# 42 of 128 attention heads with token-major scores, weights turned by DMA, and value products emitted four iterations later

## The chip, the core and the metric

The kernel runs on one NeuronCore of a Trainium2 chip. The metric is the device time of one execution in microseconds (us), the median of three runs; the profile comes from one more execution with the hardware profiler on.

TensorE (PE) multiplies; its weight loads are listed apart as PEld. ScalarE (ACT) evaluates functions, VectorE (DVE) does elementwise work, GpSimd (POOL) a little more of that, and SyncE (SP) issues nearly all DMAs. Each engine works its instructions off in the order in which the program emits them, and waits where a semaphore has not yet been reached.

## What is computed

The reference is one transformer block with adaptive layer norm. x has 2048 tokens of 1024 features; there are 32 query heads and 4 key/value heads of 128 features; keys and values are the last 512 of a cache of 2048.

```
mod = silu(c) @ w_mod                         # six vectors: sa, ca, ga, sb, cb, gb
h = layernorm(x) * (1 + ca) + sa
q = h @ wq                                    # 32 heads
p = softmax(q @ k.T * 128 ** -0.5)            # k, v: last 512 cached, one for 8 query heads
x = x + ga * ((p @ v) @ wo)
h = layernorm(x) * (1 + cb) + sb
x = x + gb * ((silu(h @ w_gate) * (h @ w_up)) @ w_down)      # 3584 wide
```

All matrices are bf16.

## The kernel before

The tokens are worked off in four chunks of 512. The attention loop (line 903) has a counter i that runs over chunk and head together: 128 heads in all, number n being head n mod 32 of chunk n div 32. It is a software pipeline written out by hand. Iteration i emits

- `qproj(i+3)` (L641): eight matmuls of 512 columns into PSUM bank 4, then a VectorE cast of the result to bf16 (L644),
- `scores(i-1)` (L805): four matmuls with 128 keys stationary and 512 queries moving, into banks 0 to 3, so that the scores lie keys by queries; then two exponentials of 128x1024 on ScalarE (L813) into one of two buffers `ex_s`,
- `pv(i-2)` (L816): 16 matmuls of 129 columns, with 128 keys x 128 queries of the exponentials stationary and 128 value columns plus a column of ones moving. The column of ones gives the sums. VectorE takes their reciprocal (L831) and multiplies (L834); a DMA transpose of 128x512 (L837) puts the head's output, features by tokens, into `oT_all`,
- one step of background work (`run_bg`): the layer norm of the next chunk, with a DMA transpose of 128x1024 for each 128 tokens (L454).

When the last head of a chunk is through, `oproj` (L870) multiplies `oT_all` by wo: eight groups of 32 matmuls, with the residual added by VectorE through two buffers `tmp` (L853, L855). Tables of iteration numbers (LOADX, LOADO, LOADT and so on, from L891) say when loads and small steps are issued; `LOADT` issues 24 DMA transposes of columns of w_mod (L588), and `load_wq` the 1 MB of weights for the next four heads. After the attention come the feed-forward layers, untouched by the change.

Waits are not written by hand. Every instruction goes through `T.op` (L55), which looks at the buffers (`_Buf`) that it reads and writes: a reader waits for the buffer's last write, and a writer for its last write and the reads since then. "Last" is by the order in which the program emits. The instruction that waits holds up its engine's queue.

All matrix products of the kernel go through a helper at L271.

Of the kernel before, what the change touches and what calls it, by code (L numbers as in the profile page):

```python
# [7 lines left out]
P = 128  # L8
# [122 lines left out]
def bass_adaLN_cond__sliding_block_cached__swiglu_ffn__prompt_kernel(  # L131
# [63 lines left out]
    rstd = [rstd4[:, i:i + 1] for i in range(4)]  # L195
    bq = S_("bq", [P, 8], F32)
    rl = [S_("rl%d" % i, [P, 4], F32) for i in range(2)]
    nsc = [S_("nsc%d" % i, [P, D], BF16) for i in range(2)]
    tmp = [S_("tmp%d" % i, [P, 512], F32) for i in range(2)]

    KB = 1024
    A_BYTES = 162 * KB
# [19 lines left out]
    def bank(b, n=512, off=0):  # L222
        return ps[:, b * 512 + off:b * 512 + off + n]
# [19 lines left out]
    B_mv = [_Buf("mv%d" % i) for i in range(4)]  # L243
    B_rs = [_Buf("rs%d" % i) for i in range(4)]
    B_rl = [_Buf("rl%d" % i) for i in range(2)]
    B_ns = [_Buf("ns%d" % i) for i in range(2)]
    B_tmp = [_Buf("tmp%d" % i) for i in range(2)]
    B_h2 = [[_Buf("h2_%d_%d" % (s, dt)) for dt in range(DT)] for s in range(2)]
# [12 lines left out]
    with nc.Block() as block:  # L261

        @block.gpsimd
        def _(g):
# [5 lines left out]
            def mm(out_ap, lhsT, rhs, start, stop, reads, bank_buf, skip=False):  # L270
                T.op(PE, lambda: TE.matmul(out_ap, lhsT, rhs, start=start, stop=stop, skip_group_check=skip),  # L271
                     reads=reads, writes=[bank_buf])
# [368 lines left out]
            def qproj(i, b=QB, k0=0):  # L641
                qproj_mm(i, b, k0, DT)
                qs = q_slot(i)
                T.op(DVE, lambda: V.tensor_copy(qT_s[qs], bank(b)), writes=[PB[b], B_qT[qs]])  # L644
# [160 lines left out]
            def scores(i):  # L805
                ch, h = divmod(i, Hq)
                gk = h // rep
                qs = q_slot(i)
                es = i % NEX
                for kt in range(KT):  # L810
                    mm(bank(SCB + kt), kT_sb[:, gk * KT + kt, :], qT_s[qs], True, True, [B_kT[gk], B_qT[qs]], PB[SCB + kt])
                for kp in range(KT // 2):
                    T.op(ACT, lambda: A.activation(ex_s[es][:, 2 * kp:2 * kp + 2, :], banks2(SCB + 2 * kp), AF.Exp, scale=att_scale),  # L813
                         writes=[PB[SCB + 2 * kp], PB[SCB + 2 * kp + 1], B_ex[es]])

            def pv(i):  # L816
                ch, h = divmod(i, Hq)
                gk = h // rep
                es = i % NEX
                os_ = i % NOS  # L820

                for jj in range(2):
                    for kt in range(KT):
                        for jb in range(2):
                            j = 2 * jb + jj
                            b = PVB + jb
                            mm(bank(b, P + 1, jj * 130), ex_s[es][:, kt, j * P:(j + 1) * P], v_aug[:, gk * KT + kt, 0:P + 1],
                               kt == 0, kt == KT - 1, [B_ex[es], B_va, B_vg[gk]], PB[b])
                both = [PB[PVB], PB[PVB + 1]]
                r = i % 2  # L830
                T.op(DVE, lambda: V.reciprocal(rl[r][:, :].rearrange("p (a b) -> p a b", a=2), psap(PVB * 512 + P, [[512, 2], [130, 2]])),  # L831
                     writes=both + [B_rl[r]])
                rlb = bass.AP(tensor=rl[r][:, :].tensor, offset=0, ap=[[4, P], [2, 2], [1, 2], [0, P]])
                T.op(DVE, lambda: V.tensor_tensor(o_s[os_].rearrange("p (a b) d -> p a b d", a=2),  # L834
                                                  psap(PVB * 512, [[512, 2], [130, 2], [1, P]]), rlb, ALU.mult),
                     reads=[B_rl[r]], writes=both + [B_os[os_]])
                T.op(Q_tr[os_], lambda: SP.dma_start_transpose(oT_all[:, h, :].rearrange("p (j q) -> p j q", j=TPC),  # L837
                                                               o_s[os_].rearrange("p j d -> p (j d)")),
                     reads=[B_os[os_]], writes=[B_oT[h]])

            B_wo = [_Buf("wo%d" % i) for i in range(8)]
            wo_s = [None] * 8
# [21 lines left out]
            def oproj_end(ch, k, b):  # L864
                j, hf = divmod(k, 2)
                t = ch * TPC + j
                resid(b, t, hf * 512, 512, 0, k, x_res[:, t, :], B_x[t])
                run_bg(1)

            def oproj(ch):  # L870
                for k in range(2 * TPC):
                    b = [QB, XB][k % 2]
                    oproj_mm(ch, k, b, 0, Hq)
                    oproj_end(ch, k, b)

            ln1 = {}
            ln2 = {}
# [15 lines left out]
            GATER = {19 + n: NGP + n for n in range(DT - NGP)}  # L893
            GATET = {23: 0, 24: 1}
            GATES = {26: 0, 27: 1}
            t2 = Hq + 6 + (9 * (NL - 1)) // 4
            TURNT = (28, t2 + 1)
            PUTT = {33: (0, c_sil, B_csil), 30: (1, mrow[0:DT, :], B_mrow), t2 + 3: (2, mrow[0:DT, :], B_mrow)}
            GETT = {35: (0, sc_row, B_scr), 31: (1, rowb[0][:, :], B_row[0]), t2 + 4: (2, rowb[1][:, :], B_row[1])}
            LOADT = {Hq + 2 + (9 * n) // 4: n for n in range(NL)}  # L900
            LOADO = {5 + (21 * p) // 8: p for p in range(8)}
            LOADK = {1: 1, 5: 2, 6: 3}
            for i in range(1, NA + 2):
                ch, h = divmod(i, Hq)
                if i in LOADK:
                    load_k(LOADK[i])
                if i == 4:
                    load_wq((i + 4) // 4 + 1)
                if 2 <= i < NQ0:
                    q_shifted(i)  # L910
                if i in (2, 3):
                    load_wga(i - 2)
                if i in LOADX:
                    load_x(LOADX[i])
                if i in LOADO:
                    load_wo(LOADO[i])
                if i in GATET:
                    gate_turn(GATET[i])
                if i in TURNT:
                    if i > Hq:  # L920
                        T.op(DVE, lambda: V.tensor_copy(mstg[:, 0:DT], mcol[:, 2 * DT:3 * DT]), reads=[B_mcol], writes=[B_mstg])
                    row_turn()
                if i in PUTT:
                    row_put(*PUTT[i])
                if i in GETT:
                    row_get(*GETT[i])
                if i == 7:
                    add_ln1(1)
                if h == 2 and 1 <= ch < NCH - 1:
                    add_ln1(ch + 1)  # L930
                if h == 2 and ch == NCH - 1:
                    add_ln2(0)
                if i + LEAD < NA:
                    if (i + LEAD) % Hq == 0:
                        finish(ln1[(i + LEAD) // Hq])
                    if i == 1:
                        scores(0)
                    if i in (1, 3, 5):
                        q_bias_mm(i + 1, i + 3, XB)
                    if i > NQ0:  # L940
                        qproj(i + LEAD)
                    elif i % 2 == 1:
                        qproj_mm(NQ0 + i // 2, QB, 0, HK)
                    else:
                        qproj(NQ0 - 1 + i // 2, QB, HK)
                if i - 4 in LOADT:
                    n = LOADT[i - 4]
                    mod_col(n)
                    g0, last = divmod(n, DT)
                    if last == DT - 1:  # L950
                        mod_take(g0, B_late[g0 + 1])
                        if g0 == 1:
                            mod_gain(1, B_late[2], B_g[1])
                n = i - (NA - LEAD)
                if 0 <= n <= 2:
                    oproj_mm(NCH - 1, 0, QB, 8 * n, 8 * n + 8)
                elif n >= 3:
                    oproj_mm(NCH - 1, 1, XB, 8 * (n - 3), 8 * (n - 3) + 8)
                if 1 <= i - 1 < NA:
                    scores(i - 1)  # L960
                if 0 <= i - 2 < NA:
                    pv(i - 2)
                    ch2, h2 = divmod(i - 2, Hq)
                    if i % 4 == 1 and i > 5:
                        load_wq((i + 4) // 4 + 1)
                    if i in LOADT:
                        load_mt(LOADT[i])
                    if h2 == Hq - 1 and ch2 < NCH - 1:
                        oproj(ch2)
                run_bg(1)  # L970
                for n in GATEP.get(i, ()):
                    gate_part(n)
                if i in GATER:
                    gate_row(GATER[i])
                if i in GATES:
                    gate_sum(GATES[i])
                if i == max(GATER):
                    gate_split()
# [152 lines left out]
```

## Time and profile before

| | before |
|---|---|
| median of 3 runs | 1270.05 us (1269.99 to 1270.45) |
| the profiled execution, its own time | 1270.14 us |
| its span, first to last instruction | 1268.3 us |
| TensorE busy | 1255.1 us (99%) |
| VectorE busy | 485.1 us (38%) |
| ScalarE busy | 341.6 us (27%) |
| DMA transposes of heads (128x512), to landing, median | 2.6 us |
| DMA transposes of the layer norm (128x1024), to landing, median | 5.1 us |

The profile is a page and answers drawn from the same trace. A line of a group reads: source line, engine, operation, out<-in by the program's names, shapes, count; then busy time and mean time of one in ns; then the idle time of the engine just before, with what ended it. A timeline line reads: start and duration in us, engine, line, operation, count, and in brackets the idle time before it. Of a DMA the line gives the duration of its issue on the queue (SPq is SyncE's), and apart from that the time from issue to landing. Matmuls are pipelined, so their mean durations are longer than their distance. A few matmul records can be missing.

### The profile page before, as it was taken

To read this page: it belongs to the slowest core of one execution; us is meant where nothing else is said; L and a number is where in the kernel's file an instruction comes from. 1 tells how busy PE (TensorE), PEld (TensorE's weight loads), DVE (VectorE), ACT (ScalarE), POOL (GpSimd) and SP (SyncE) were. 2 spreads that over 40 slices of the span, in tenths; PEclk is the share of its full clock that TensorE was granted. 3 is DMA by queue.
4 is the path that set the end of the run, shared out by engine and by line. 5 is a ranking of instruction groups with operands and counts; after the bars stand their busy time and mean duration, and the time that the engine had idled before them with its cause. 6 is when DMAs were issued, how large, how long until landed. Compare 5 with 4: busy or idle time off the path is not lost.

```text
span 1268.3 us, 17609 instructions
## 1 busy us (share of the span) xinstructions
PE 1255.1 (99%) x7442; PEld 640.7 (51%) x7583; DVE 485.1 (38%) x894; ACT 341.6 (27%) x389; POOL 56.0 (4%) x95
## 2 busy tenths in 40 slices
PE   8999999999999999999999999999999999999999
PEld 5655545555455554555544444444444444444444
DVE  4676226764257641365322321233212321222122
ACT  4655205553035550155510111011100111011100
POOL 1530000000000000000000000000000000000000
PEclk9999999999999999999999999999999999999999
DMA  9998306875029641064243972055512644034200
GB/s 320 264 263 218 92 1 127 177 171 125 1 57 177 138 114 34 9 129 123 61 145 100 291 246 94 25 158 150 168 40 72 177 141 134 17 128 154 67 9 25
DMA packets 239997, 156.67 MB, mean 124 GB/s; under 512 B 133296, under 2 KB 225840, under 8 KB 239920
## 3 DMA queue, kind: packets, MB, share of 16 engines
q1 hardware_dynamic: 181664, 96.83, 31.6%
q10 hardware_dynamic: 58256, 58.73, 14.6%
q8 instruction: 59, 0.97, 0.3%
q14 instruction: 18, 0.15, 0.1%
HBM read 119.93 MB, written 4.20 MB: 98 GB/s over the span
## 4 chain that ended last, share of the span: by engine, by line
PE 98%; issue 1%; DMA 0%; SPq 0%; DVE 0%
PE ps L271 98%; DMA arena<-in_w_mod_dram 0%; SPq L309 0%; SPq L334 0%; PE ps L275 0%; DVE arena L496 0%; DVE tmp L853 0%; DVE arena L855 0%; DVE gain_f L486 0%
## 5 line engine op out<-in xcount | busy, mean ns | idle before, releaser
L271 PE MATMUL ps<-arena 128*128 128x512 bf16 (+1 forms) x7213 | 1249.3, 333 | 10.1 <-POOL arena L298 2.0
L271 PEld LDWEIGHTS ps<-arena 128*128 128x128 bf16 x7354 | 632.9, 98 | 621.5 <-issue 2.1
L813 ACT ACTIVATE arena<-ps 128x1024 bf16<-128x1024 f32 x256 | 261.9, 1023 | 345.1 <-PE ps L271 333.4
L1059 ACT ACTIVATE arena<-ps 128x512 bf16<-128x512 f32 x112 | 66.9, 597 | 499.6 <-PE ps L271 499.6
L1060 DVE TENSOR_TENSOR arena<-ps,arena 128x512 bf16<-128x512 f32 x112 | 77.5, 692 | 276.2 <-PE ps L271 276.2
L853 DVE TENSOR_TENSOR tmp<-ps,rowb 128x512 f32<-128x512 f32 (+1 forms) x65 | 44.4, 683 | 318.8 <-PE ps L271 318.8
L644 DVE CAST arena<-ps 128x512 bf16<-128x512 f32 x120 | 82.8, 690 | 47.7 <-PE ps L271 47.7
L834 DVE TENSOR_TENSOR arena<-ps,rl 128x512 bf16<-128x512 f32 x128 | 88.5, 691 | 4.7 <-DVE rl L831 0.2
L831 DVE RECIPROCAL rl<-ps 128x4 f32<-128x4 f32 x128 | 23.4, 182 | 114.1 <-PE ps L271 114.1
L429 POOL TENSOR_SCALAR rstd<-mv 128x1 f32<-128x1 f32 x28 | 6.1, 216 | 910.3 <-DVE mv L428 910.3
L424 DVE BATCH_NORM_STATS2 st<-x_res 128x6 f32<-128x512 bf16 x62 | 42.4, 683 | 3.4 <-DMA x_res<-in_A_x_dram 3.3
L593 DVE SCALAR_TENSOR_TENSOR arena<-arena 128x1024 bf16<-128x1024 bf16 x24 | 29.2, 1215 | 0.0
L855 DVE TENSOR_TENSOR arena<-tmp,x_res 128x512 bf16<-128x512 f32 (+2 forms) x33 | 22.3, 677 | 1.1
L855 DVE TENSOR_TENSOR x_res<-tmp,x_res 128x512 bf16<-128x512 f32 x32 | 22.2, 693 | 1.1
L440 DVE TENSOR_SCALAR arena<-arena,gain,mod_bf 128x512 bf16<-128x512 bf16 x56 | 21.2, 420 | 0.0
L435 DVE TENSOR_SCALAR nsc<-x_res,mv,rstd 128x1024 bf16<-128x1024 bf16 x30 | 19.2, 641 | 0.0
L431 POOL TENSOR_TENSOR rstd<-rstd,mhalf 128x1 f32<-128x1 f32 x28 | 15.7, 559 | 2.3
L772 POOL TENSOR_SCALAR arena<-arena,sc_bf 128x512 f32<-128x512 bf16 x8 | 12.9, 1614 | 0.5 <-POOL arena L774 0.2
L774 POOL TENSOR_TENSOR arena<-arena 128x512 f32<-128x512 f32 x8 | 10.1, 1265 | 0.7
L428 DVE BATCH_NORM_AGGREGATE mv<-st 128x2 f32<-128x12 f32 x28 | 5.8, 209 | 1.0
L271 PEld LDWEIGHTS ps<-sc_bf,arena 128*128 128x128 bf16 x128 | 4.4, 96 | 1.4 <-DMA arena<-in_w_mod_dram 0.3
L271 PE MATMUL ps<-sc_bf,arena 128*128 128x1 bf16 x128 | 4.7, 164 | 0.3 <-DMA arena<-in_w_mod_dram 0.3
(56 smaller groups left out, 59.4 us busy)
## 6 DMA issues: line engine op xcount, KB each, us to landing
arena<-in_A_wq_dram SPq DMA_DIRECT2D x30, 1024.0 KB, 5.8
arena<-in_B_w_gate_dram ACTq DMA_DIRECT2D x28, 1024.0 KB, 5.4
arena<-in_B_w_up_dram ACTq DMA_DIRECT2D x28, 1024.0 KB, 7.9
arena<-in_A_wo_dram SPq DMA_DIRECT2D x8, 1024.0 KB, 7.6
arena<-in_B_w_down_dram SPq DMA_DIRECT2D x7, 1024.0 KB, 8.3
out_dram<-arena SPq DMA_DIRECT2D x15, 256.0 KB, 2.0
x_res<-in_A_x_dram SPq DMA_DIRECT2D x3, 1024.0 KB, 7.0
arena<-arena SPq DMA_TRANSPOSE x132, 2.6
```

Source lines behind the costliest of these rows:

```text
L271: T.op(PE, lambda: TE.matmul(out_ap, lhsT, rhs, start=start, stop=stop, skip_group_check=skip), reads=reads, writes=[bank_buf])
L424: T.op(DVE, lambda: V.bn_stats(st_[sl][:, hf * 6:hf * 6 + 6], x_res[:, t, hf * 512:hf * 512 + 512]), reads=[B_x[t]], writes=[B_st[sl]])
L440: T.op(DVE, lambda: V.tensor_scalar(dst[:, dt, :], dst[:, dt, :], gain[gi][:, dt:dt + 1], mod_bf[:, ccol + dt:ccol + dt + 1], op0=ALU.mult ...
L593: T.op(DVE, lambda: V.scalar_tensor_tensor(mt[n % 2], mt[n % 2], 1.0, sc_row, op0=ALU.mult, op1=ALU.mult, accum_out=mcol[:, n:n + 1]), rea ...
L644: T.op(DVE, lambda: V.tensor_copy(qT_s[qs], bank(b)), writes=[PB[b], B_qT[qs]])
L813: T.op(ACT, lambda: A.activation(ex_s[es][:, 2 * kp:2 * kp + 2, :], banks2(SCB + 2 * kp), AF.Exp, scale=att_scale), writes=[PB[SCB + 2 * k ...
L831: T.op(DVE, lambda: V.reciprocal(rl[r][:, :].rearrange("p (a b) -> p a b", a=2), psap(PVB * 512 + P, [[512, 2], [130, 2]])), writes=both + ...
L834: T.op(DVE, lambda: V.tensor_tensor(o_s[os_].rearrange("p (a b) d -> p a b d", a=2), psap(PVB * 512, [[512, 2], [130, 2], [1, P]]), rlb, A ...
L853: T.op(DVE, lambda: V.tensor_tensor(tmp[s][:, 0:n], bank(b, n), rowb[ri][:, c0:c0 + n], ALU.mult), reads=[B_row[ri]], writes=[PB[b], B_tmp ...
L855: T.op(DVE, lambda: V.tensor_tensor(dst[:, c0:c0 + n], tmp[s][:, 0:n], x_res[:, t, c0:c0 + n], ALU.add), reads=[B_tmp[s], B_x[t]], writes= ...
L1059: T.op(ACT, lambda: A.activation(sg_s[ss], bank(gb), AF.Silu), writes=[PB[gb], B_sg[ss]])
L1060: T.op(DVE, lambda: V.tensor_tensor(guT[:, ft, :], bank(ub), sg_s[ss], ALU.mult), reads=[B_sg[ss]], writes=[PB[ub], B_gu[ft]])
```

## The change

42 of the 128 heads take another form: numbers 34, 36 to 54, and 66, 68 to 126. All are even; the odd ones between them stay as they were.

For such a head (`nat_scores`) the queries are stationary and 512 keys move, so the scores lie queries by keys. Four exponentials of 128x512 write the buffer `pn[s]` and, with an accumulator, the sums of each row. `nat_norm` takes reciprocals and multiplies in place, in two halves. `nat_turn` issues one DMA transpose of 128x2048 from `pn[s]` to `pt[s]`. `nat_pv` then has the values stationary and 512 queries moving: four matmuls, whose result is already features by tokens; ScalarE copies it to `oT_all`. There are two slots: `p_slot(i) = (i - 34) // 2 % 2`. Slot 0 of `pn` lies where `ex_s[0]` lay, slot 1 is the `tmp` pair of the residual. The slots of `pt` lie in a region that changes at heads 34, 66, 86 and 96 (`PTAT`).

In the loop, `nat_scores(i+1)` and the first half of its `nat_norm` stand in the odd iteration i, the second half and `nat_turn` in the next one, and `nat_pv(i-4)` behind that. At a chunk's end what is left is flushed before `oproj`. Heads 34, 66 and 98 have their scores and normalisation between groups of `oproj`. `load_wq` moves ahead of the scores from iteration 33 on, the w_mod transposes go to every second iteration (from nine in four), and the background step moves ahead of `nat_scores` in odd iterations.

```diff
+            NAT0 = Hq + 2
+            NAT = set(range(NAT0, 2 * Hq - 8, 2)) | set(range(2 * Hq + 2, NA, 2))
+            B_pn = [[_Buf("pn0_%d" % hf) for hf in range(2)], B_tmp]
+            pn = [None, tmp_t[:, :].bitcast(BF16)]
...
+            def p_slot(i):
+                return (i - NAT0) // 2 % 2
...
+            def nat_scores(i):
...
+                for j in range(TPC):
+                    mm(bank(SCB + j), qT_s[qs][:, j * P:(j + 1) * P],
+                       kT_sb[:, gk * KT:(gk + 1) * KT, :].rearrange("p a b -> p (a b)"), True, True,
+                       [B_kT[gk], B_qT[qs]], PB[SCB + j])
+                for j in range(TPC):
+                    T.op(ACT, lambda: A.activation(pn[s][:, j * 512:(j + 1) * 512], bank(SCB + j), AF.Exp, scale=att_scale,
+                                                   accum_out=psum[s][:, j:j + 1]),
+                         writes=[PB[SCB + j], B_pn[s][j // 2], B_psum[s][j // 2]])
+            def nat_norm(i, hf):
+                s = p_slot(i)
+                T.op(DVE, lambda: V.reciprocal(pinv[s][:, 2 * hf:2 * hf + 2], psum[s][:, 2 * hf:2 * hf + 2]),
+                     reads=[B_psum[s][hf]], writes=[B_pinv[s][hf]])
+                for j in (2 * hf, 2 * hf + 1):
+                    pj = pn[s][:, j * 512:(j + 1) * 512]
+                    T.op(DVE, lambda: V.tensor_scalar(pj, pj, pinv[s][:, j:j + 1], None, op0=ALU.mult),
+                         reads=[B_pinv[s][hf]], writes=[B_pn[s][hf]])
+            def nat_turn(i):
+                s = p_slot(i)
+                pt_of[i] = (pt[s], B_pt[s], list(pt_over))
+                T.op(Q_pt[s], lambda: SP.dma_start_transpose(pt[s], pn[s]), reads=B_pn[s], writes=[B_pt[s]])
+            def nat_pv(i):
...
+                pa, pb, over = pt_of.pop(i)
+                ptv = pa.rearrange("p (j k) q -> p j k q", j=TPC)
+                for kt in range(KT):
+                    mm(bank(PVB).rearrange("p (j q) -> p j q", j=TPC), v_aug[:, gk * KT + kt, 0:P], ptv[:, :, kt, :],
+                       kt == 0, kt == KT - 1, [B_va, B_vg[gk], pb], PB[PVB])
+                T.op(ACT, lambda: A.activation(oT_all[:, h, :], bank(PVB), AF.Copy), writes=[PB[PVB], B_oT[h]])
...
+            PTAT = {NAT0: OFF_OT + 24 * KB, 2 * Hq + 2: OFF_OT + 24 * KB, 2 * Hq + 22: OFF_H20, 3 * Hq: OFF_HT}
...
+                if i % 4 == 1 and i >= NAT0 - 1:
+                    load_wq((i + 4) // 4 + 1)
...
+                seam = (i - 1) % Hq == 0 and i + 1 in NAT
+                if i + 1 in PTAT and not seam:
+                    pt_region(PTAT[i + 1])
+                if i in NAT and (i - 2) % Hq:
+                    nat_norm(i, 1)
+                    nat_turn(i)
+                nat = i % 2 == 1 and i + 1 in NAT
+                if nat and not seam:
+                    if i - 4 not in LOADT:
+                        run_bg(1)
+                    nat_scores(i + 1)
+                if 1 <= i - 1 < NA and i - 1 not in NAT:
                     scores(i - 1)
                 if 0 <= i - 2 < NA:
-                    pv(i - 2)
+                    if i - 4 in pt_of:
+                        nat_pv(i - 4)
+                    if i - 2 not in NAT:
+                        pv(i - 2)
+                    if (i - 2) % Hq == Hq - 1 or i == NA:
+                        for n in sorted(pt_of):
+                            if n < i:
+                                nat_pv(n)
+                    if nat and not seam:
+                        nat_norm(i + 1, 0)
...
                     if h2 == Hq - 1 and ch2 < NCH - 1:
-                        oproj(ch2)
+                        oproj(ch2, [lambda: nat_scores(i + 1), lambda: (nat_norm(i + 1, 0), nat_norm(i + 1, 1))] if seam else ())
+                        if seam:
+                            if i + 1 in PTAT:
+                                pt_region(PTAT[i + 1])
+                            nat_turn(i + 1)
```

## The prediction

> **What bounds the kernel now.** I read the page's busy table first, then its chain of waits, then the timeline of two quiet iterations of the attention loop.
>
> ```profile
> span 1268.3 us, 17609 instructions
> ...
> PE 1255.1 (99%) x7442; PEld 640.7 (51%) x7583; DVE 485.1 (38%) x894; ACT 341.6 (27%) x389; POOL 56.0 (4%) x95
> ...
> PE 98%; issue 1%; DMA 0%; SPq 0%; DVE 0%
> ```
>
> TensorE is busy for 99% of the span and carries 98% of the chain: it never waits in the attention loop. So an edit gains only by giving TensorE less to do, and every wait put on TensorE's queue is paid in full. The timeline gives the pace.
>
> ```profile
> 597.79 0.69 DVE L834 TENSOR_TENSOR arena<-ps,rl 128x512 bf16<-128x512 f32 x1
> ...
> 598.51 1.19 SPq L837 DMA_TRANSPOSE arena<-arena  x1
> 599.30 0.69 DVE L644 CAST arena<-ps 128x512 bf16<-128x512 f32 x1 [0.82 <-PE ps L271]
> 599.73 2.14 ACT L813 ACTIVATE arena<-ps 128x1024 bf16<-128x1024 f32 x2 [1.36 <-PE ps L271]
> ...
> 601.07 0.18 DVE L831 RECIPROCAL rl<-ps 128x4 f32<-128x4 f32 x1 [1.08 <-PE ps L271]
> 601.28 0.69 DVE L834 TENSOR_TENSOR arena<-ps,rl 128x512 bf16<-128x512 f32 x1
> ...
> 602.80 0.69 DVE L644 CAST arena<-ps 128x512 bf16<-128x512 f32 x1 [0.82 <-PE ps L271]
> ```
>
> One iteration is 3.50 us (602.80 - 599.30, from one cast of projected queries to the next). SyncE issues a transpose 0.03 us after VectorE is done (598.51 after 597.79 + 0.69).
>
> The pace of TensorE comes from the chain in order of time and, for its start, from the timeline of TensorE:
>
> ```profile
> 472.40 10.74 PE ps L271 x49
> ```
>
> ```profile
> 2.02 1.03 PE L271 MATMUL ps<-arena 128*128 128x512 bf16 x2 [2.02 <-POOL arena L298]
> 2.99 0.18 PE L510 MATMUL ps<-arena,c_row 8*128 8x8 bf16 x1
> 3.10 4.34 PE L271 MATMUL ps<-arena 128*128 128x512 bf16 x12
> ```
>
> A 128x512 matmul takes 0.219 us in a steady run (10.74 / 49). The first ones, after 2.02 us of idleness, take 0.36 us (4.34 / 12), though the granted clock stands at 1.00 in those slices.
>
> **What TensorE saves.** For 42 heads, 16 value products of 129 columns become four of 512. An iteration has 12 other matmuls of 512 columns; 12 x 0.219 = 2.63 us leaves 0.87 us for the 16. Four cost 0.88 us. With missing records the 0.219 is a little high, so the difference lies between 0 and 0.05 us a head; I take 0.05, 2 us in all. The four score products have the same columns as before.
>
> **The wait.** In an even iteration J the change emits, in this order: the query projection of head J+3, nat_norm(J, 1), nat_turn(J), the scores of head J-1, nat_pv(J-4). nat_turn(J) writes the slot pt[p_slot(J)]. With two slots and every second head, p_slot(J) = p_slot(J-4): it is the slot that nat_pv(J-4) is about to read. The tracker makes a reader wait for the slot's last write in program order, which by then is nat_turn(J). So the products do not use a transpose four iterations old: they wait for the one issued in their own iteration (and read head J's weights). That transpose can't start before VectorE has cast head J+3's queries, which waits for TensorE, and normalised the second half of head J.
>
> Behind the waiting matmul, in order on TensorE, stand the next projection, the next scores, the next old-form products: everything. ScalarE and VectorE run dry behind them. The durations:
>
> ```profile
> L834 DVE TENSOR_TENSOR arena<-ps,rl 128x512 bf16<-128x512 f32 x128 | 88.5, 691 | 4.7 <-DVE rl L831 0.2
> ...
> L831 DVE RECIPROCAL rl<-ps 128x4 f32<-128x4 f32 x128 | 23.4, 182 | 114.1 <-PE ps L271 114.1
> ...
> L675 DVE TENSOR_SCALAR arena<-arena,mod_bf 128x512 bf16<-128x512 bf16 x8 | 2.2, 348 | 0.0
> ```
>
> The new multiply is a bf16 multiply in place of 128x512 by one scalar a partition, as L675 is an add: 0.35 us. A nat_norm half is 0.18 + 2 x 0.35 and about 0.03 before each: 0.97 us. No transpose of 128x2048 is in the trace. The nearest are 128x512 (L837) and 128x1024 (L454), each in a quiet stretch:
>
> ```profile
> L837 SPq DMA_TRANSPOSE arena<-arena x13: 1189/1190/1844, 598.5 to 639.6; - x13
> ...
> DMA to landing us min/median/max: 2.4/2.5/3.9
> ```
>
> ```profile
> L454 SPq DMA_TRANSPOSE arena<-nsc x2: 1247/1254/1262, 540.3 to 550.8; - x2
> ...
> DMA to landing us min/median/max: 3.1/3.1/3.1
> ```
>
> 512 columns more cost 0.67 us, so 2048 land after 3.1 + 2 x 0.67 = 4.45 us. Bounds: 3.1 us from below; from above 2 x 3.1 = 6.2 us if it went by bytes without a fixed part. I take 4.45, in line with both rows.
>
> Now count from the start of iteration J. Old-form products of head J-3 have just ended; VectorE spends 0.97 us on their reciprocal and multiply and 0.97 us on nat_norm(J, 0): 1.94. The projection ended at 8 x 0.219 = 1.75, so the cast runs 1.94 to 2.63, nat_norm(J, 1) to 3.60, the transpose is issued at 3.63 and lands at 8.08. TensorE ended its scores at 12 x 0.219 = 2.63. It stands idle for about **5.5 us**. In chunk 1 and early in chunk 2 the w_mod transposes (24 as before, now every second iteration; 4.3 us median) are issued about 3 us ahead of it on SyncE and still move for up to 1 us: 5.7 us on average.
>
> How often: where the slot of J-4 is rewritten in iteration J. Heads 34 to 50 (9), 66 to 80 (8), 86 to 90 (3), 98 to 122 (13): **33**. Heads 52, 54, 124 and 126 have no successor; 82, 84 and 92 are spared because pt moves to another region. Head 96, flushed at iteration 97, waits some 1 us for a transpose one iteration old. 33 x 5.7 + 1 = 189 us.
>
> **After the wait.** TensorE restarts after 5.5 us of rest. The nearest row is the kernel's start: its first 14 large matmuls end at 7.44, 5.42 us after 2.02, where 14 x 0.219 = 3.07 are due: a loss of 2.3 us. Bounds per wait: 0 and 2.3 us. I take the middle, 1.2 us, because a rest of 5.5 us is more than twice the 2.02 us that preceded the slow start, but comes out of a warm run: 33 x 1.2 = 40 us.
> [...]
>
> **What costs nothing, and its cover.** Four exponentials of 512 with sums take 4 x (0.60 + 0.19) = 3.2 us (L1059; the accumulator read at L518 is 187 ns) against 2.05 us: with the other head's 2.05 and a 0.6 us copy ScalarE has 5.9 us in a pair of iterations of 7.0. VectorE has two casts, one old-form pair, two nat_norm halves and a step of layer norm, some 4.9 us in 7.0. Both fit if TensorE sets the pace, with no room for more than 1 us beside. The moved weight load (0.53 us on SyncE) opens an odd iteration; its 5.8 us are over before the transpose of the even one is issued 7 us later. Score products of heads 34, 66 and 98 between output projections are moved work; the tmp buffers that slot 1 shares are free by then. 42 old transposes and multiplies go, none on the path. A layer-norm step issues after nat_turn, in the wait.
>
> **Sum.** Against the profiled execution's own 1270.14 us (span 1268.3 and 1.8 around it; the median of the runs is 1270.05, the same): 1270 - 2 + 189 + 40 = **1497 us**.
>
> **Rivals.**
> - *The pace does not fall after a wait* (chance 0.18). For it: the clock row reads 1.00 throughout. 1270 - 2 + 189 = 1457 us.
> - *The pace falls as at the start each time, or transposes land late* (0.14). For it: the start's row. 33 x 2.3 = 76: 1533 us. With landings at 6.2 us instead of 4.45, 33 x 1.75 = 58 more: 1591. [...]
> - *The products do not wait for their own iteration's transpose* (0.06): the other side, not slower. It holds if the slot they read was last written four iterations earlier; then the 4.45 us landing lies within 14 us and only the saving stays: 1268 us. It turns on one thing, whether nat_turn(J) stands ahead of nat_pv(J-4) on the same slot. The point from which it decides: products one iteration after their transpose (at 3.50 + 2.63 = 6.1 us, landing at 8.1) would still wait 2 us, products two iterations after it (9.6 us) not at all. I read the order in the code as plain, hence the low chance.
>
> **Chances.** The forecast, waits with some loss of pace, 0.62; rivals 0.18, 0.14, 0.06. A measurement of this kernel can tell about 0.2%, 2.5 us, from no change; 1268 lies within that, or just beyond. So faster 0.02, same 0.03, slower 0.95. The range: from waits of 5.3 us (33 x 5.3 = 175) without loss, 1443 us, to 5.7 + 2.3 with an eighth on top for late landings (33 x 9.0 = 297), 1565 us: 1440 to 1570.
>
> **What would show it.** Among the waits, the weight load or matmul of TensorE waiting for the DMA transpose from tmp or arena, 33 times at 5 to 6 us; TensorE busy for six or seven tenths in the slices of these heads, and for nine and more, as now, in the output projections and in the feed-forward half; landings of 4.4 to 5 us; pairs of iterations of 12.5 us or more; granted clock below 1 in those slices if pace is lost. It is wrong if TensorE waits for the transposes of four iterations earlier, if the landing is below 4 or over 6 us, or if ScalarE is what TensorE waits for.

## The result, and the profile after

The changed kernel takes 1527.11 us (median of 6 runs, 1524.38 to 1528.67) against 1270.1 us: a ratio of the means of 1.2016, 95% interval 1.2001 to 1.2032. The profiled execution took 1527.75 us with a span of 1526.0 us. Its page, in the lines that answer to those of before:

```profile
span 1526.0 us, 17303 instructions
...
PE 1327.5 (87%) x7079; PEld 630.9 (41%) x7079; DVE 514.5 (34%) x1062; ACT 391.0 (26%) x683; POOL 55.9 (4%) x95
...
PE   9999974659995657898566689999999999999999
...
PEclk9999987789998889999898899999999999999999
...
PE 79%; DMA 10%; DVE 9%; issue 1%; SPq 1%; ACT 0%; ACTq 0%
```

The span grew by 257.7 us. TensorE is idle for 198.5 us (1526.0 - 1327.5) where it was for 13.2, and *busy* for 72.4 us more, though it has fewer columns to stream. Both lie in the slices of the token-major heads; the feed-forward half is as before. The clock row, all nines before, shows sevens and eights in those slices. DMA and VectorE, with 0% of the chain before, have 19% of it.

The waits by line (engine and line that waited, what for; us in total, times, longest):

```profile
PE ps L276 <- DMA arena<-arena: 101.6, 18, 7.8
...
PE ps L276 <- DMA arena<-tmp: 84.7, 15, 9.6
```

18 + 15 = 33 waits, 186.3 us. The line of the turn (L896 is `nat_turn`) shows who waits for it and when it lands:

```profile
L896 SPq DMA_TRANSPOSE arena<-arena x22: 1521/1934/4277, 194.9 to 878.5; - x22
L896 SPq DMA_TRANSPOSE arena<-tmp x20: 1741/1976/5847, 205.4 to 865.5; - x20
...
  PE ps L276: 186.4, 33
...
DMA to landing us min/median/max: 4.2/4.4/7.9
```

One of these waits in the timeline:

```profile
782.04 0.69 DVE L649 CAST arena<-ps 128x512 bf16<-128x512 f32 x1
782.47 2.14 ACT L820 ACTIVATE arena<-ps 128x1024 bf16<-128x1024 f32 x2 [0.89 <-PE ps L276]
782.65 0.15 DVE L886 RECIPROCAL pinv<-psum 128x2 f32<-128x2 f32 x1
782.84 0.74 DVE L890 TENSOR_SCALAR tmp<-tmp,pinv 128x512 bf16<-128x512 bf16 x2
783.61 1.95 SPq L896 DMA_TRANSPOSE arena<-tmp  x1
...
787.98 4.63 PE L276 MATMUL ps<-arena 128*128 128x512 bf16 x14 [5.12 <-DMA arena<-tmp]
...
792.22 0.69 DVE L649 CAST arena<-ps 128x512 bf16<-128x512 f32 x1 [8.64 <-PE ps L276]
```

The cast of projected queries, the second half of the normalisation, the turn, and then a rest of TensorE: the products start when the turn lands, at 787.98, 4.37 us after its issue, and the next cast comes 10.18 us after the last one instead of 3.50. The stretches of that pair of iterations (us, TensorE busy and matmuls, weight loads, VectorE, ScalarE, GpSimd, granted clock, DMA share, GB/s):

```profile
773.86:777.27 3.41, 2.99 (x8) 1.07 (x9) 0.00 (x0) 0.60 (x1) 0.00 (x0) 0.50 0.00 0
777.27:787.51 10.24, 5.59 (x38) 2.85 (x36) 3.78 (x10) 4.69 (x10) 0.00 (x0) 1.00 0.36 67
787.51:790.92 3.41, 2.94 (x7) 1.01 (x8) 0.00 (x0) 0.60 (x1) 0.00 (x0) 0.50 0.95 294
```

In the 3.41 us after a wait TensorE does seven or eight matmuls at a granted clock of 0.50. There are 33 such falls of the clock in the trace, one for each wait, 164 us in all. For 121 us of these 164 TensorE has a matmul in flight. Matmuls of 128x512 start 0.43 us apart between 787.98 and 790.92, at 0.50, and 0.22 us apart after 792.4, at 1.00. If all that work took half as long at the full clock, some 61 us are lost to the pace by this estimate, 1.8 us a wait.

### The profile page after: what moved, and what is told of

Its sections match the earlier page's. It is cut to its first block, busy times and chain, and to the rows that moved or that the text cites. A ratio compares the mean times of both kernels' runs of the same rounds, so it can differ in the third digit from the quotient of the medians.

```text
span 1526.0 us, 17303 instructions
## 1 busy us (share of the span) xinstructions
PE 1327.5 (87%) x7079; PEld 630.9 (41%) x7079; DVE 514.5 (34%) x1062; ACT 391.0 (26%) x683; POOL 55.9 (4%) x95
## 4 chain that ended last, share of the span: by engine, by line
PE 79%; DMA 10%; DVE 9%; issue 1%; SPq 1%; ACT 0%; ACTq 0%
PE ps L276 79%; DMA arena<-arena 6%; DMA arena<-tmp 5%; DVE arena L649 2%; DVE arena L841 2%; DVE arena L890 2%; DVE tmp L890 1%; DVE arena L598 1%; SPq L593 1%; DVE st L429 0%; DVE rl L838 0%; DVE pinv L886 0%; ACT arena L820 0%; DMA x_res<-in_A_x_dram 0%; DVE nsc L440 0%
## 5 line engine op out<-in xcount | busy, mean ns | idle before, releaser
L276 PE MATMUL ps<-arena 128*128 128x512 bf16 (+2 forms) x6850 | 1322.3, 357 | 195.4 <-DMA arena<-arena 101.6
L276 PEld LDWEIGHTS ps<-arena 128*128 128x128 bf16 x6850 | 623.3, 100 | 888.7 <-DMA arena<-arena 111.4
L820 ACT ACTIVATE arena<-ps 128x1024 bf16<-128x1024 f32 x172 | 176.0, 1023 | 251.5 <-PE ps L276 243.6
L1159 ACT ACTIVATE arena<-ps 128x512 bf16<-128x512 f32 x112 | 66.9, 597 | 500.2 <-PE ps L276 500.2
L907 ACT ACTIVATE arena<-ps 128x512 bf16<-128x512 f32 x42 | 25.0, 596 | 197.7 <-PE ps L276 197.7
L880 ACT ACTIVATE arena<-ps 128x512 bf16<-128x512 f32 x88 | 52.1, 595 | 61.5 <-PE ps L276 57.7
L841 DVE TENSOR_TENSOR arena<-ps,rl 128x512 bf16<-128x512 f32 x86 | 59.5, 691 | 3.2 <-DVE rl L838 0.2
L880 ACT ACTIVATE tmp<-ps 128x512 bf16<-128x512 f32 x80 | 47.4, 595 | 42.6 <-PE ps L276 38.9
L838 DVE RECIPROCAL rl<-ps 128x4 f32<-128x4 f32 x86 | 15.7, 182 | 81.4 <-PE ps L276 81.4
L890 DVE TENSOR_SCALAR arena<-arena,pinv 128x512 bf16<-128x512 bf16 x88 | 31.1, 353 | 3.1
L890 DVE TENSOR_SCALAR tmp<-tmp,pinv 128x512 bf16<-128x512 bf16 x80 | 28.3, 353 | 2.8
L880 ACT ACTIVATION_READ_ACCUMULATOR arena<-ps 128x1 f32 x88 | 17.3, 196 | 0.0
```

Source lines behind the costliest of these rows:

```text
L880: T.op(ACT, lambda: A.activation(pn[s][:, j * 512:(j + 1) * 512], bank(SCB + j), AF.Exp, scale=att_scale, accum_out=psum[s][:, j:j + 1]), ...
L890: T.op(DVE, lambda: V.tensor_scalar(pj, pj, pinv[s][:, j:j + 1], None, op0=ALU.mult), reads=[B_pinv[s][hf]], writes=[B_pn[s][hf]])
L1159: T.op(ACT, lambda: A.activation(sg_s[ss], bank(gb), AF.Silu), writes=[PB[gb], B_sg[ss]])
```

## The experiments

Theory after the result: the products wait for the turn of their own iteration, because it is the last write of the slot that they read (so head J-4's values are multiplied with head J's weights), and each wait also costs a stretch at half pace. Rivals: the token-major form itself is slow; the slow matmuls come from its operands. All ratios are of mean times, against the kernel before on the same chip.

**The order put right.**

```diff
-                if i in NAT and (i - 2) % Hq:
-                    nat_norm(i, 1)
-                    nat_turn(i)
...
                     if i - 4 in pt_of:
                         nat_pv(i - 4)
+                    if i in NAT and (i - 2) % Hq:
+                        nat_norm(i, 1)
+                        nat_turn(i)
```

> Edit: in an even iteration the second half of the normalisation and the turn of head J are emitted behind the value products of head J-4 instead of ahead of them; nothing else moves, and each head is multiplied with its own weights. Theory (the products wait for the turn of their own iteration because it is the last write of the slot they read): all 33 waits of TensorE go, and the loss of pace with them; 1268 to 1271 us, with at most the 1 us at the flush of iteration 97 left. Rival (the token-major form itself is slow: long transposes, ScalarE or VectorE too full, strided moving operand): most of the 257 us stays, over 1400 us.

1284.48 us, ratio 1.0113 (1.0096 to 1.013). The granted clock is 1.00 throughout, and of TensorE's waits for a transpose one is left (in all, times, longest):

```profile
PE ps L276 <- DMA arena<-arena: 0.3, 1, 0.3
```

Moving three lines takes 243 us away, so the wait is shown to be an effect of the order. The expectation missed all the same: 14 us stay over the kernel before, not 0. In a quiet stretch the form does what was forecast:

```profile
588.78 0.69 DVE L649 CAST arena<-ps 128x512 bf16<-128x512 f32 x1 [1.91 <-PE ps L276]
...
592.27 0.69 DVE L649 CAST arena<-ps 128x512 bf16<-128x512 f32 x1
...
595.73 0.69 DVE L649 CAST arena<-ps 128x512 bf16<-128x512 f32 x1 [1.91 <-PE ps L276]
```

Two iterations take 6.95 us instead of 7.00. I compared the time of every query cast with that of the same head before: the 14 us come in steps, 8.6 between heads 46 and 62, and most of the rest at the chunk seams.

**Two iterations on instead of four** (`nat_pv(i - 4)` becomes `nat_pv(i - 2)`; the order stays as in the change).

> Edit: the value products come two iterations after the turn instead of four, the order inside the iteration is left as the change has it; the two slots then suffice, since the turn of head J writes the other slot. Theory: products at 9.6 us against a landing at 8.1 us after the start of the iteration of the turn, so no wait in most heads; where the transposes of w_mod or the weight load are in the way, up to 1 us; 1268 to 1285 us. Rival (form itself slow): over 1400 us.

1288.86 us, ratio 1.0144 (1.0129 to 1.016), just above the expected band. TensorE's waits for transposes are 11, with 12.6 us in all, and two falls of the clock are left. At a distance that two slots allow, the same order does no great harm.

**One iteration on.**

```diff
-                    if i - 4 in pt_of:
-                        nat_pv(i - 4)
                     if i - 2 not in NAT:
                         pv(i - 2)
+                    if i - 1 in pt_of:
+                        nat_pv(i - 1)
```

> Edit: the value products come one iteration after the turn, behind the old-form products of the odd iteration. Theory: a wait of some 2.0 us for each of the 42 heads (landing at 8.1 us, products at 3.45 + 2.63 - 0.88 + 0.87 = 6.1 us): 84 us. The rests are shorter than the 3.4 us steps in which the clock changes, so the granted clock stays at 1.00: 1268 + 84 = 1352 us, 1340 to 1375. Rival on the loss of pace (each rest costs its 2.2 us whatever its length): 1352 + 92 = 1444 us.

1360.02 us, ratio 1.0692 (1.0665 to 1.072): within the theory's band, far from the rival's 1444. But the mechanism was only half right, and the band was met in part by luck. The rests come to some 68 us where 84 were expected; most are 1.4 to 1.7 us long and leave the clock alone. Seven falls came all the same, and made up a part. This one followed a rest of 1.97 us:

```profile
257.38:260.79 3.41, 1.44 (x19) 1.10 (x18) 3.29 (x9) 2.46 (x8) 0.77 (x2) 1.00 1.01 223
260.79:264.20 3.41, 3.41 (x9) 1.18 (x9) 0.00 (x0) 0.60 (x1) 0.00 (x0) 0.50 0.58 115
```

TensorE was busy for 1.44 us of the 3.41 us before that fall, and then did nine matmuls in 3.41 us. A rest of 2.92 us near the end of the attention part (it ends at 709.62) left the clock alone, so in this run the length of a rest does not decide by itself.

**The wait filled with matmuls.**

```diff
                     if i - 4 in pt_of:
+                        if i in NAT and pt_of[i - 4][1] is B_pt[p_slot(i)]:
+                            for _ in range(20):
+                                mm(bank(PVB + 1), kT_sb[:, 0, :], kT_sb[:, 0:KT, :].rearrange("p a b -> p (a b)"), True, True,
+                                   [B_kT[0]], PB[PVB + 1])
                         nat_pv(i - 4)
```

> Edit: the changed kernel, with 20 more matmuls of 128x512, whose result nobody reads, put on TensorE ahead of each of the 33 value products that wait. Theory on the loss of pace (TensorE is slowed after resting over 3.4 us): the rest shrinks from 5.6 to 1.3 us, the granted clock stays at 1.00, the 4.3 us lie inside the wait: 1527 - 71 = 1456 us, although it does more. Rival (the slow matmuls come from the new operands or from the transposes that run beside them, not from the rest): 1527 us or more.

1476.47 us, ratio 1.1621 (1.1604 to 1.1638). With 660 matmuls more the kernel is 51 us *faster* than the changed one. Four falls of the clock are left of 33. So here the half pace comes from the rest, and not from the operands or from the transposes that run beside. The expectation was 20 us too low in the main because it took nearly all of the added busy time, 71 us, for loss of pace. By the half-speed stretches the loss is 61 us, and the four falls that are left keep 7 of it by the same estimate; the difference, 54, is close to the 51 found.

**A quarter of each head turned** (128x512 instead of 128x2048; three quarters of the weights are left out of these products).

```diff
+                    T.op(POOL, lambda: g.memset(pt[s], 0.0), writes=[B_pt[s]])
...
-                T.op(Q_pt[s], lambda: SP.dma_start_transpose(pt[s], pn[s]), reads=B_pn[s], writes=[B_pt[s]])
+                T.op(Q_pt[s], lambda: SP.dma_start_transpose(pt[s][:, 0:KT, :], pn[s][:, 0:KT * P]), reads=B_pn[s], writes=[B_pt[s]])
```

> Edit: the changed kernel, but of each head's weights only the first quarter (128x512 instead of 128x2048) is turned; the other three quarters of pt keep zeros, written once by GpSimd when the region is taken, so three quarters of the weights are left out of the value products. Same number of matmuls, same order, same 33 waits. Theory: the landing falls from 4.4 to 2.4 us, so each wait falls by 2.0 us to 3.6 us (33 x 2.0 = 66 us less). A rest of 3.6 us seldom holds a whole step of 3.4 us, so most of the loss of pace (71 us) goes too: 1527 - 66 - 60 = 1400 us, 1385 to 1425. Rival on the loss of pace (any wait costs 2.2 us): 1527 - 66 = 1461 us. Rival on the wait (the landing isn't its last part): 1527 us.

1462.48 us, ratio 1.1496 (1.1448 to 1.1545).

```profile
  PE ps L276: 123.6, 33
...
DMA to landing us min/median/max: 2.4/2.4/6.2
```

The waits fell by 62.8 us, as the theory of the wait had it (66). The loss of pace stayed, as the rival had it: 25 of the 33 rests, most of them 3.2 to 3.8 us, end in a fall. Here the stretch before one such fall and the three after it:

```profile
557.17:560.58 3.41, 1.20 (x6) 0.35 (x4) 1.81 (x6) 2.05 (x2) 0.00 (x0) 1.00 0.99 180
560.58:563.99 3.41, 2.42 (x6) 0.89 (x7) 0.00 (x0) 0.49 (x1) 0.00 (x0) 0.50 0.12 23
563.99:567.41 3.42, 3.42 (x9) 1.21 (x8) 0.50 (x1) 0.18 (x2) 0.00 (x0) 0.50 0.00 0
567.41:570.82 3.41, 3.41 (x29) 2.06 (x28) 1.90 (x7) 2.57 (x8) 0.06 (x1) 1.00 0.00 0
```

This rest was 3.2 us. After a stretch with TensorE busy for 35% (1.20 of 3.41 us) the clock fell; after the next, busy for 71%, it had not come back; after the one busy throughout, it had. My theory of the loss, which the expectations of one on, of the filled wait and of this run take as known (a rest must hold a whole step of 3.4 us), was an estimate and does not stand: no run shows such a bound. What the traces showed is in the last section.

**The moves alone** (`NAT = set()`: no head token-major).

> Edit: the changed kernel with no head in the token-major form; what is left is the earlier weight load, the w_mod transposes at every second iteration and the moved background steps. Theory (these cost nothing): 1270 us, within 1 us. Rival (they bring part of the 14 us by which the kernel with the order put right is over the kernel before): up to 1284 us.

1270.5 us, ratio 1.0 (0.9991 to 1.0009). The earlier weight load and the w_mod transposes at every second iteration cost nothing. The move of the background step is not tested here: with `NAT` empty the step stays at the end of each iteration.

**Order and flush** (besides the order, `if n < i:` becomes `if n < i - 1 or i == NA:`; in the change, head 96 is flushed into `oT_all` before the output projection of the chunk before it has read that place).

> Edit: as the kernel with products ahead of the turn, and the flush at a chunk's end leaves the head of the next chunk (96) to its own iteration. Of the 14 us over before, the trace of that kernel has 2.6 us in the flush at iteration 97, where old-form products, head 94 and head 96 follow each other through PSUM bank 5 and TensorE waits for each eviction (1.1, 0.8, 0.7 us). Theory: one of the two flushed heads goes and 0.7 to 1.5 us with it: 1283 us. Rival (the flush costs nothing): 1284.5 us.

1281.89 us, ratio 1.0094 (1.0081 to 1.0108). The casts of projected queries show where the gain of some 2 us over the kernel with the order alone comes from: between heads 100 and 104 that kernel falls 3.2 us behind the kernel before, this one 1.3.

**Without the second chunk's heads** (`NAT = set(range(2 * Hq + 2, NA, 2))`, otherwise as the last).

> Edit: as the kernel with order and flush put right, with the 11 heads of the second chunk left in the old form (31 heads token-major). In the second chunk the w_mod transposes, the loads of x and the weight loads share SyncE and the DMA engines with the turns, and the trace of the kernel with the order put right is 8.6 us behind there. Theory (the loss is made by turns that stand in the queue with those loads): 1283 - 8.6 + 0.5 = 1275 us. Rival (each token-major head costs a little everywhere): 31/42 of the 13 us stay, 1280 us.

1276.36 us, ratio 1.0046 (1.0033 to 1.0058): the theory's 1275, not the rival's 1280. The 11 heads of the second chunk carry about half of what is lost.

**Where the second chunk loses.** Windows of 20 iterations in chunks 1, 2 and 3, first of the kernel before, then of the one with order and flush right (columns as above; the last three are clock, DMA share, GB/s):

```profile
198.57:268.50 69.93, 69.41 (x551) 41.59 (x560) 49.40 (x100) 40.92 (x40) 3.10 (x8) 1.00 0.81 171
379.70:449.64 69.94, 69.42 (x551) 41.59 (x560) 48.23 (x101) 40.93 (x40) 2.31 (x6) 1.00 0.76 154
550.35:620.28 69.93, 69.41 (x551) 41.59 (x560) 37.57 (x77) 40.92 (x40) 1.54 (x4) 1.00 0.49 110
```

```profile
200.20:276.40 76.20, 70.94 (x440) 35.80 (x439) 56.17 (x139) 50.86 (x109) 3.11 (x8) 1.00 0.98 198
391.60:463.00 71.40, 69.69 (x441) 36.37 (x440) 52.44 (x133) 51.75 (x110) 2.10 (x5) 1.00 1.05 212
564.90:634.30 69.40, 69.40 (x441) 36.39 (x440) 44.02 (x116) 51.78 (x110) 1.54 (x4) 1.00 0.83 166
```

ScalarE and VectorE stay under 57 of 76 us. The DMA share goes from 0.81 to 0.98 and from 0.76 to 1.05: the turns fill the DMA engines. From 200 to 292 us TensorE waits 3.3 us for weights that come late, and 3.2 us for banks that the exponentials have not yet emptied. But the share alone does not tell the loss: chunk 2 has the higher one and loses 1.5 us, chunk 1 6.3. The next run makes the turns smaller and leaves the work of ScalarE and VectorE as it was.

**Order and flush, a quarter turned** (three quarters of the weights left out again).

> Edit: as the kernel with order and flush put right (42 heads), but only the first quarter of each head's weights is turned, as in the earlier run with a quarter; three quarters of the weights are left out of the products. ScalarE, VectorE and TensorE have the same work. Theory (the 9.7 us lost in the second chunk come from the turns' own load on SyncE and on the DMA engines, whose share there is 0.98 against 0.81 before): most of them go; the seams' 3 to 4 us stay: 1274 us, 1272 to 1277. Rival (ScalarE or VectorE too full there): 1282 us.

1275.05 us, ratio 1.004 (1.0027 to 1.0052), as the theory said. In chunk 1 only 1.3 us are lost between heads 46 and 62 instead of 9.8, and the DMA share there is 0.81 (196 to 266 us) instead of 0.98. So the size of the turns is what cost the second chunk, and not the work of ScalarE or VectorE. Whether it binds through SyncE's queue, through the DMA engines or through the later landing of each turn stays open, as the run changes all three.

**Only heads in quiet stretches** (`NAT` = 72 to 82 and 104 to 126; the region of head 66 taken at 72).

> Edit: as the kernel with order and flush put right, but only heads 72 to 82 and 104 to 126 token-major (18), none of them at a chunk's seam and none in the second chunk. Theory (a token-major head saves 0.05 us where nothing else is short; the 11 us above came from seams, from the loads of the second chunk and from the flush): 1270.5 - 18 x 0.05 = 1269.6 us, 1269 to 1272. Rival (every such head costs a little): 1270.5 + 18 x 0.3 = 1276 us.

1277.49 us, ratio 1.0057 (1.0043 to 1.007). Both expectations missed. Inside the stretches a pair takes 6.95 us as before, but entering a stretch in mid-chunk costs 2.7 us: that iteration holds the scores of two heads. The timeline of TensorE and ScalarE there:

```profile
552.00 0.60 ACT L880 ACTIVATE tmp<-ps 128x512 bf16<-128x512 f32 x1 [1.14 <-PE ps L276]
...
552.78 0.60 ACT L880 ACTIVATE tmp<-ps 128x512 bf16<-128x512 f32 x1
...
553.52 0.39 PE L276 MATMUL ps<-arena 128*128 128x512 bf16 x1 [0.39 <-ACT tmp L880]
554.10 0.39 PE L276 MATMUL ps<-arena 128*128 128x512 bf16 x1 [0.19 <-ACT tmp L880]
```

TensorE goes from one exponential to the next, since both heads want banks 0 to 3. Leaving the first stretch cost 2.5 us more. No version tried is faster than the kernel before: 42 x 0.05 = 2 us are to be had, and one entrance costs more.

## Why the prediction was right, and what it missed

- *The order and the wait*: right. 33 waits were named and 33 counted, and the run with the order put right shows the cause. The landing of the unseen 128x2048 transpose came out at 4.4 us (4.45 extrapolated from the two smaller ones). 189 us were priced and 186.4 measured, and that closeness is partly luck: most waits of the last chunk are 5.0 to 5.1 us where 5.5 were counted, and the first waits of the chunks, four in all, are about 7 to 9.6.
- *The saving*: right. 0.05 us a head; 6.95 for 7.00 us a pair.
- *The pace after a wait*: that a wait costs pace was right, the size was not. 1.2 us a wait, 40 us, were taken as the middle of 0 and 2.3; the half-speed stretches give 1.8 us, 61 us in all. That is 21 of the 30 us by which the forecast fell short. TensorE's busy time grew by 72.4 us, but not all of it is pace: with the order put right it is 10 us above the kernel before at the full clock. The rival with the start's loss at every wait (76 us) was the nearer guess. The row that it rests on was read wrongly, as slow matmuls at a granted clock of 1.00: the trace of the kernel before has no clock record ahead of 6.32 us, so that 1.00 was not measured. Until then most matmuls start 0.43 us apart, from 6.4 us on 0.22, so the start shows the half pace too (0.43 us is the distance at 0.50 in the changed kernel).
- *What was left out of the sum*: 1270 - 2 + 186 + 61 = 1515, 12 us under the measured time. The casts fall behind by 6.6 us at the chunk seams and where the token-major heads of chunk 1 end, terms that the prediction put at nothing; some 5 us stay unattributed.
- *What costs nothing*: the moved loads do cost nothing. The turns do not: SyncE issues one in 1.9 us (median) where the nearest row had 1.25, and they fill the DMA engines in two chunks (share 0.98 and 1.05 with order and flush right, 0.81 and 0.76 before). I had looked at the landing of a turn and not at how long it occupies the engines. In the changed kernel this part is hidden: its trace has no wait of TensorE for the query weights in these chunks, and the DMA share is 0.55 from 200 to 292 us and 0.49 from 460 to 560. With the order right it is about half of the 14 us: with a quarter turned the kernel is 6.8 us faster.
- *The rival on the other side* (1268 us, products that do not wait): the order decides it, as it said; but with the order right the time is 1284 and not 1268, so its price was wrong by the last two terms.

## What to carry to other kernels

A buffer ring of n slots allows a reader at most n - 1 turns behind the writer when the writer is emitted first; one step more and a tracker that knows only the last write turns the prefetch into a wait for the newest transfer, and into a read of its contents. Price a rest of TensorE by its length, and look in the trace for a stretch at half pace behind it: here the 33 rests took 5.6 us each on average, and by estimate 1.8 us more went after each, while most rests of 1.4 to 1.7 us in the run with one on left the clock at 1.00. And of a new transfer count not only the landing (here 4.4 us) but its share of the DMA engines in the busiest stretch (here 0.98 and 1.05 with the turns, 0.81 and 0.76 before).

## What the runs showed of the hardware

In five traces (the changed kernel, two on, one on, filled, quarter turned) the granted clock changed only at whole multiples of 3.41 us, counted from the first clock record of the trace. I took all such stretches and the share of each in which TensorE had a matmul in flight (the ends of matmuls are modelled, so the shares are the profile's). All 71 falls (33, 2, 7, 4 and 25) followed a stretch with a share of 0.42 or less. No full-clock stretch up to 0.39 was without one, and four between 0.40 and 0.42 were. All 71 returns to full clock followed a share of 0.79 or more, and shares up to 0.77 left it low. In the changed kernel alone the 33 falls followed shares of 0.27 or less and full-clock stretches of 0.47 or more none; at the low clock 0.76 was the highest share without a return and 0.79 the lowest with one. So the one rest of 1.97 us above, where 1.44 of 3.41 us were busy, was enough. 40 of the 71 falls followed a stretch that was not wholly idle; in the changed kernel it is 7 of 33.

In the changed kernel this locks: the last 12 falls followed each other at 13.65 us, four stretches.

A 128x2048 transpose within SBUF landed after 4.4 us (median in the changed kernel), 128x1024 after 3.1 and 128x512 after 2.4 (quiet stretches of the kernel before; 2.4 also with a quarter turned). The three fit 0.67 us for 512 columns on top of 1.75 us, by estimate.
